# A gated linear recurrence with a tanh-shrink layer behind it: seven products for the second dense product, engine orders from a list scheduler, two heads computed in place for two units

## The chip, the cores and the metric

The kernel runs on one core of one Trainium2 chip. A core has five engines, each with an instruction queue of its own that it works off in order: TensorE (matmuls; in the profile PE, and PEld for its weight loads), VectorE (DVE), ScalarE (ACT), GpSimd (POOL) and SyncE (SP, which here only starts DMA transfers). TensorE writes its results into eight banks of PSUM; everything else lives in SBUF, with 128 partitions. The metric is the time of one execution on the device, in microseconds (us); the shorter, the better.

## What is computed

The reference has two stages. The first is a recurrence over 768 time steps for 4 batches and 8 heads with 48 features each; the second is a dense layer on the result.

```python
for t in range(S):                                   # S = 768, state is 48 x 48 per head
    state = alpha[t][:, None] * state + outer(k[t], v[t])
    y[t] = q[t] @ state
x = y, transposed to (3072 tokens, 384 features)     # 8 heads x 48
h = x @ w_in                                         # 384 x 2048
g = h - tanh(h)
out = g @ w_out                                      # 2048 x 384
```

q, k, v and alpha are 32-bit floats; w_in and w_out arrive as 64-bit floats. The output has 3072 x 384 32-bit floats.

## The kernel before

**Units and steps.** The 3072 tokens are cut into 12 units of 256 tokens; three units make up a batch. A unit has two chunks of 128 tokens. For every unit the kernel runs the recurrence (`gla`) and the dense layer (`moe`); the dense layer of a unit is cut into 8 steps of 256 hidden features each.

**The recurrence of a unit.** alpha, k and q are loaded (`load`, issued at line 362) so that VectorE can turn them with 32 x 32 transposes (`flip`, line 381) into tiles with features on the partitions: two heads share the 128 partitions, at partitions 0 to 47 and 64 to 111. A head's 48 features need two 32-partition blocks, so each tensor is loaded twice, the second time shifted by 32 elements. VectorE then makes two running products of the decays: a backward scan U (line 395) and a forward scan W (line 411), with some small operations in between (lines 403 to 405). GpSimd multiplies k by U and q by W (line 417), and ScalarE sums the squares of U and W as a check of their size (line 427). For each chunk TensorE multiplies q and k to scores (line 451), VectorE masks them (458), and TensorE makes y out of the old state and the masked scores (472, 476). ScalarE copies y into the layer's input xT (483, 484). xT has 384 rows without gaps, three blocks of 128. y's two-head groups fill only 96 of 128 partitions, so the rows of the last two heads go to a tile xs and from there, by six small DMA transfers (`moves`, line 523), into the gaps of the other three groups' rows. For the next chunk's state TensorE turns k back (492), ScalarE copies it (497), TensorE makes the update (503), GpSimd decays the old state (463), and VectorE adds both (512, or 510 in the first chunk of a batch).

**A step of the layer.** `first` (line 534) makes h for 256 hidden features and 256 tokens: six products with 128 x 128 weights and 256 columns, each two instructions. h - tanh(h) is a polynomial in u = h squared, which ScalarE and VectorE share: ScalarE makes u and two squares of linear functions of it (lines 542 to 544), VectorE w = h u, then z1 and g (545 to 547), and ScalarE accumulates how far u exceeds the range in which the polynomial is valid (549). `second` (line 558) multiplies g by w_out: for each of two feature blocks and two token chunks one product with 384 columns, summed over the 8 steps in two PSUM banks. At the unit's end ScalarE copies the two sums (564) and SyncE stores them. At the very end flags are checked; if a range was left, a slower general routine computes everything again.

**The weights.** They are loaded in 16 pieces (8 of w_in, 8 of w_out) of 768 columns, and rounded from 64 to 32 bits in `round_weight`: two ScalarE operations (lines 61, 62), three on VectorE (65, 67, 69) and one addition on GpSimd (72). At most four raw pieces are held at a time. Unit 0's steps can only run as pieces come in.

**What sets the order.** Every piece of work is put into a list with a time written out by hand (`put(at, ...)`): one table of times for unit 0, one for unit 1, one relative table for all others, and a step every 6.6 us. The list is sorted by these times, and the instructions are issued in that order; each engine's queue is thus fixed, and semaphores alone decide when an instruction runs. `first` of a step stands 2.5 steps ahead of its `second`.

**PSUM.** Two banks hold scores, one y, one the turned-back k and the update, two h, two the sums of `second`.

Of the kernel before, what the change touches and what calls it, by code (L numbers as in the profile page):

```python
# [8 lines left out]
FP32 = mybir.dt.float32  # L9
# [7 lines left out]
P = 128  # L17
HP = 64
# [239 lines left out]

def fast(tc, q, k, v, alpha, moe_w_in, moe_w_out, out, w_in, w_out, ident, ok, pad_rows):
# [11 lines left out]
    EV = HP + D  # L271
# [5 lines left out]
    with ExitStack() as ctx:  # L277
# [4 lines left out]
        ps_y = ctx.enter_context(tc.tile_pool(name="ps_y", bufs=1, space=PSUM))  # L282
        ps_h = ctx.enter_context(tc.tile_pool(name="ps_h", bufs=2, space=PSUM))
        ps_o = ctx.enter_context(tc.tile_pool(name="ps_o", bufs=1, space=PSUM))


# [10 lines left out]
        raws = [consts.tile([P, NP, R, D], FP32, name=n) for n in ("ar", "kr", "qr")]  # L297
        for t, x in zip(raws, (1.0, 0.0, 0.0)):
            V.memset(t[:, :, R - 1, :], x)


# [5 lines left out]
        for t in (after, before):  # L307
            GP.memset(t, 0.0)
        low = consts.tile([P, N], FP32, name="low")
        GP.memset(low, 1.0 / R_MAX)  # L310
        GP.memset(after[:, P::P + 1], 1.0)
        states = [consts.tile([P, NP, EV], FP32, name=f"state{i}") for i in range(2)]
# [3 lines left out]
        raw_in, raw_out = {}, {}  # L316

        def fetch_in(s):
            parts = []
            for i in range(len(pad_rows[0])):  # L320
                at, f0 = pad_rows[0][i]
                step = pad_rows[1][i][1] - f0
                src = moe_w_in[f0:f0 + KT * step].rearrange("(j p) n -> p j n", p=step)
                parts.append((at, src[0:at.stop - at.start, :, 2 * s * P:2 * (s + 1) * P]))
            raw_in[s] = load_weight(nc, two, parts)

        def fetch_out(s):
            raw_out[s] = load_weight(nc, two, [(slice(0, P), w_out_r[:, 2 * s:2 * s + 2, :])])

        def round_in(s):  # L330
            return round_weight(nc, two, raw_in.pop(s), w_in[:, :, 2 * s * P:2 * (s + 1) * P])

        def round_out(s):
            return round_weight(nc, two, raw_out.pop(s), w_out[:, 2 * s:2 * s + 2, :])


        plan = []

        def put(at, do, *args):
            plan.append((at, len(plan), do, args))  # L340

        def convert(at, make, s):

            it = []
            put(at, lambda: (it.append(make(s)), next(it[0])))
            put(at + 1, lambda: next(it[0]))
            put(at + 3, lambda: next(it[0], None))
# [3 lines left out]
        def load(u):  # L351
            b, i = divmod(u, UPB)
            t0 = i * TU
            other = A if u == 0 else nc.sync
            for n, (t, x) in enumerate(zip(raws, (alpha, k, q))):
                queue = other if n == 1 else nc.sync
                for hh in range(2):
                    src = x[b].rearrange("(g two) s d -> two g (s d)", two=2)[hh][:, t0 * D:(t0 + TU) * D]
                    src = src.rearrange("g (i n) -> i g n", i=32)
                    for dq in range(2):  # L360
                        at = 64 * hh + 32 * dq
                        queue.dma_start(
                            out=t[at:at + 32].rearrange("p g r d -> p g (r d)")[:, :, 0:R * D - 32 * dq],
                            in_=src[:, :, 32 * dq:])
            vt = vts[u] = three.tile([P, CU, H, D], FP32, name="vt")
            for c in range(CU):
                other.dma_start(out=vt[:, c], in_=v[b, :, t0 + c * P:t0 + (c + 1) * P, :].rearrange("h p d -> p h d"))

        def gla(u, at):

# [5 lines left out]
            m = {}  # L376

            def flip(raw, make):
                t = make()
                for g in range(NP):  # L380
                    V.transpose(t[:, g].rearrange("p c (i r) -> p r c i", r=R), raw[:, g, :, 0:32])  # L381
# [4 lines left out]

            put(at["aT"], flip, raws[0], lambda: tail[:, :, 0:P].rearrange("p (g c) t -> p g c t", c=CU))
            put(at["kT"], flip, raws[1], lambda: new("kT"))
            put(at["qT"], flip, raws[2], lambda: new("qT"))

# [6 lines left out]
            put(at["U"], scan_U)  # L397
# [8 lines left out]
            put(at["ends"], ends)  # L406
# [6 lines left out]
            put(at["W"], scan_W)  # L413

            def scale(name, by, cs):
                t = m[name][:, :, cs]
                GP.tensor_mul(t, t, m[by].rearrange("p (g c) t -> p g c t", c=CU)[:, :, cs, 1:])  # L417
            for name, by in (("kT", "U"), ("qT", "W")):
                if u == 0:
                    for c in range(CU):  # L420
                        put(at[name + by] + c, scale, name, by, slice(c, c + 1))
                else:
                    put(at[name + by], scale, name, by, slice(0, CU))
# [8 lines left out]
            def open_x():  # L432
                m["xs"] = two.tile([P, TU], FP32, name="xs")
                xT[u] = two.tile([P, KT, TU], FP32, name="xT")
# [253 lines left out]
```

## Time and profile before

| | |
|---|---|
| median of three runs | 719.04 us (716.86 to 722.59) |
| the profiled execution | 716.62 us |
| its span, first to last instruction | 714.8 us |
| TensorE's mean granted clock | 0.975 |
| busy: TensorE, VectorE, ScalarE, GpSimd | 621.6, 451.3, 329.2, 115.9 us |
| `first` (line 534), `second` (line 558) on TensorE | 275.8, 267.0 us |
| the scan W (line 411), the transposes (line 381) on VectorE | 48.7, 73.3 us |
| read and written in HBM | 44.43 and 4.72 MB |

The page of the profile gives busy times by engine, a picture of the span in 40 slices (each digit is the busy share in tenths), DMA queues, the chain of work that ended last, and groups of instructions. A group's row reads: line, engine, operation, what it writes and reads, shapes and count; then busy time in all and mean nanoseconds of one; then the idle time of the engine ahead of it and what ended that. A row of the timeline begins with the start and the duration in us; in brackets stands the idle time ahead of it and its releaser. Matmuls are pipelined: their rows overlap, and the distance from start to start is what they cost in a stream.

### The profile page before, as it was taken

Reading aid. Unit: us, or ns where it says so; the run is one execution under the profiler, and the core shown is the slowest. Engines: PE = TensorE matmul, PEld = TensorE weight load, DVE = VectorE, ACT = ScalarE, POOL = GpSimd, SP = SyncE. Lnnn points to the kernel's source line nnn. Section 1 sums busy time; section 2 is a strip of 40 time slices with the busy share of each in tenths; the row PEclk is TensorE's granted clock in tenths of the full one; section 3 lists DMA queues with packets and bytes.
Section 4 is the critical chain, followed back from the end, with each engine's and each line's share of the span. In section 5 each row is a group of like instructions: output and inputs, shape, how many; then the busy total and the mean of one; then the engine's idle time right before and its main releaser. Section 6 shows DMA issues by size and latency. Waiting matters only on the chain.

```text
span 714.8 us, 8728 instructions
## 1 busy us (share of the span) xinstructions
PE 621.6 (87%) x3089; PEld 460.4 (64%) x3089; DVE 451.3 (63%) x639; ACT 329.2 (46%) x701; POOL 115.9 (16%) x98
## 2 busy tenths in 40 slices
PE   0655586879989989989989989989989989989995
PEld 0543365657757767767767667767767767767773
DVE  4749877783683783682783773773874864874341
ACT  1435355544544544544634534634544444444451
POOL 2522543130020030030020120030110120120000
PEclk9978799999999999999999999999999999999998
DMA  9996556300801701701702602602603503500000
GB/s 181 213 178 146 107 141 164 58 1 18 160 1 28 150 1 31 146 1 37 141 1 55 122 1 54 124 1 60 118 1 81 97 1 81 98 0 7 23 0 28
DMA packets 57268, 50.99 MB, mean 71 GB/s; under 512 B 29440, under 2 KB 52096, under 8 KB 57216
## 3 DMA queue, kind: packets, MB, share of 16 engines
q1 hardware_dynamic: 54560, 49.20, 33.0%
q10 hardware_dynamic: 2656, 1.15, 1.0%
q8 instruction: 26, 0.43, 0.3%
q14 instruction: 26, 0.21, 0.1%
HBM read 44.43 MB, written 4.72 MB: 69 GB/s over the span
## 4 chain that ended last, share of the span: by engine, by line
PE 45%; DVE 27%; DMA 15%; POOL 5%; issue 3%; ACT 2%; SPq 2%; DVEq 0%; POOLq 0%; ACTq 0%
PE h L534 21%; PE o L558 15%; DVE W L411 6%; DMA qr<-in_q_dram 6%; DMA raw<-in_moe_w_in_dram 4%; DMA ar<-in_alpha_dram 3%; PE sc L451 3%; DVE kT L381 3%; DVE qT L381 3%; DVE z L546 3%; POOL qT L417 3%; DVE U L395 3%; PE y L476 3%; DVE w L545 3%; DVE aT L381 3%
## 5 line engine op out<-in xcount | busy, mean ns | idle before, releaser
L534 PE MATMUL h<-xT,w_in 128*128 128x256 f32 x1152 | 275.8, 391 | 22.9 <-POOL w_in L72 15.3
L558 PE MATMUL o<-w_out,g 128*128 128x384 f32 x768 | 267.0, 491 | 11.4 <-POOL w_out L72 11.4
L534 PEld LDWEIGHTS h<-xT,w_in 128*128 128x128 f32 x1152 | 221.7, 195 | 72.1 <-POOL w_in L72 17.6
L558 PEld LDWEIGHTS o<-w_out,g 128*128 128x128 f32 x768 | 144.3, 191 | 95.3 <-POOL w_out L72 13.1
L542 ACT ACTIVATE u<-h 128x512 f32<-128x512 f32 x96 | 57.3, 597 | 244.2 <-PE h L534 244.2
L545 DVE TENSOR_TENSOR w<-h,u 128x512 f32<-128x512 f32 x96 | 65.6, 683 | 162.6 <-ACT u L542 162.4
L417 POOL TENSOR_TENSOR kT<-kT,U 128x1024 f32<-128x1024 f32 (+1 forms) x13 | 30.3, 2331 | 377.1 <-DVE least L404 377.1
L546 DVE SCALAR_TENSOR_TENSOR z<-z,w 128x512 f32<-128x512 f32 x96 | 83.5, 869 | 10.6 <-DVE w L545 0.9
L547 DVE SCALAR_TENSOR_TENSOR g<-z,z 128x512 f32<-128x512 f32 x96 | 67.3, 701 | 10.4 <-ACT big L549 0.5
L543 ACT ACTIVATE z<-u 128x512 f32<-128x512 f32 x96 | 60.5, 630 | 3.1
L549 ACT ACTIVATE big<-u 128x512 f32<-128x512 f32 x96 | 58.9, 614 | 0.0
L544 ACT ACTIVATE z<-u 128x512 f32<-128x512 f32 x96 | 58.9, 613 | 0.0
L411 DVE TENSOR_TENSOR_SCAN W<-aT,before 128x1032 f32<-128x1032 f32 x12 | 48.7, 4059 | 0.4
L458 DVE TENSOR_TENSOR pm<-sc,mask 128x512 f32<-128x512 f32 x46 | 29.6, 685 | 16.9 <-PE sc L451 16.5
L503 PE MATMUL up<-vt,kn 128*128 128x96 f32 x160 | 22.8, 287 | 18.8 <-ACT kn L497 18.8
L417 POOL TENSOR_TENSOR qT<-qT,W 128x1024 f32<-128x1024 f32 (+1 forms) x13 | 26.7, 2053 | 65.6 <-DVE qT L381 65.6
L451 PE MATMUL sc<-qT,kT 48*128 48x128 f32 x368 | 27.6, 291 | 10.5 <-POOL qT L417 10.5
L451 PEld LDWEIGHTS sc<-qT,kT 48*128 48x128 f32 x368 | 23.1, 193 | 20.8 <-POOL qT L417 16.7
L503 PEld LDWEIGHTS up<-vt,kn 128*128 128x128 f32 x160 | 20.8, 198 | 22.6 <-ACT kn L497 22.0
L483 ACT COPY xs<-y 48x128 f32<-48x128 f32 x48 | 12.5, 260 | 46.5 <-PE y L476 46.2
L512 DVE TENSOR_TENSOR state<-state,up 48x192 f32<-48x192 f32 x32 | 11.2, 350 | 34.7 <-PE up L503 33.4
L492 PE MATMUL tp<-ident,kT 128*128 128x128 f32 x80 | 13.2, 291 | 20.1 <-POOL kT L417 20.1
(60 smaller groups left out, 444.0 us busy)
## 6 DMA issues: line engine op xcount, KB each, us to landing
raw<-in_moe_w_out_dram SPq DMA_DIRECT2D x8, 768.0 KB, 4.6
ar<-in_alpha_dram SPq DMA_DIRECT2D x24, 192.0 KB, 3.7
qr<-in_q_dram SPq DMA_DIRECT2D x24, 192.0 KB, 6.9
raw<-in_moe_w_in_dram SPq DMA_DIRECT2D x16, 288.0 KB, 7.8
out_dram<-ob SPq DMA_DIRECT2D x24, 192.0 KB, 1.9
ar<-in_alpha_dram SPq DMA_DIRECT2D x24, 176.0 KB, 4.1
qr<-in_q_dram SPq DMA_DIRECT2D x24, 176.0 KB, 6.9
kr<-in_k_dram SPq DMA_DIRECT2D x22, 192.0 KB, 5.3
```

The costliest lines, as they stand in the source:

```text
L381: V.transpose(t[:, g].rearrange("p c (i r) -> p r c i", r=R), raw[:, g, :, 0:32])
L411: V.tensor_tensor_scan(out=W.rearrange("p n t -> p (n t)"), data0=aT[:, 0:N * (P + 1)], data1=before, initial=0.0, op0=ALU.mult, op1=ALU.add)
L417: GP.tensor_mul(t, t, m[by].rearrange("p (g c) t -> p g c t", c=CU)[:, :, cs, 1:])
L451: T.matmul(sc[hh][:, g, :], lhsT=m["kT"][q, g, c, :], rhs=m["qT"][q, g, c, :], start=True, stop=True)
L534: T.matmul(h[:, a, :], lhsT=w_in[:, j, f * P:(f + 1) * P], rhs=xT[u][:, j, :], start=(j == 0), stop=(j == KT - 1))
L543: A.activation(z1, sq, AF.Square, bias=QB1, scale=QA)
L544: A.activation(z2, sq, AF.Square, bias=QB2, scale=QA)
L545: V.tensor_mul(w, h, sq)
L546: V.scalar_tensor_tensor(out=z1, in0=z1, scalar=QK1, in1=w, op0=ALU.add, op1=ALU.mult)
L547: V.scalar_tensor_tensor(out=g, in0=z2, scalar=QK2, in1=z1, op0=ALU.add, op1=ALU.mult)
L549: A.activation(big, sq, AF.Relu, bias=-U_MAX, accum_out=over[:, n:n + 1])
L558: T.matmul(o[c], lhsT=g[:, a * TU + c * P:a * TU + (c + 1) * P], rhs=w_out[:, f, :], start=(f == 0), stop=(f == FT - 1))
```

## The change

**Seven products.** For units 2 to 11, `second` uses Strassen's scheme on 2 x 2 blocks: g is cut by its two feature blocks and its two token chunks, w_out by feature block and by halves of its 384 columns. Seven products of 192 columns take the place of four of 384 (which are eight of 192). VectorE makes the five sums of blocks of g in three operations per step (`sums`, a tile e of 5 x 128 columns). The five combinations of blocks of w_out are made once (`combine`, four on GpSimd, one on VectorE, 1536 columns each), in memory that the raw weights had held, after the last piece has been converted. The products accumulate in four PSUM banks rather than two, and the store puts the output's blocks together: one copy on ScalarE, four operations on VectorE, four half-width stores. Units 0 and 1 (`PLAIN = 2`) keep the four products.

**Engine orders.** The hand-written times are gone. Each task has a name, an engine, an estimated duration, a rank and the tasks it waits for. `Planner.order` runs a list scheduling in Python while the kernel is built: always the engine that can start earliest takes, of its ready tasks, the one with the lowest rank. The order so found is the order of issue. A unit's dense steps have ranks 16 u + 2 s, their `second` 5 more; the recurrence of unit u begins at rank 16 u - 24 (units 0 and 1 at -40 and -20).

**In place.** For units 0 and 1 the rows of the last two heads are computed by TensorE straight into the gaps of y, with weight tiles of 32 columns that hold 16 features behind 16 zeros (`v_gap`, `s_gap`); one copy then takes y to xT, and `moves` and xs aren't used.

**Loads.** alpha, k and q are loaded once; the shifted second half is a copy from partition block to block (`widen`: six ScalarE copies per unit, for unit 0's alpha one of them on VectorE).

**PSUM.** y and the turned-back k and update lose their own banks. Units 0 and 1 use two of the four sum banks for them, later units the score banks, so that a chunk's scores wait until the chunk before has been masked, copied and added to the state.

**Smaller.** Unit 0's products of k with U and q with W go from GpSimd to VectorE; an early activation loads ScalarE's table; 36 and later 7 products of the identity matrix with itself keep TensorE busy ahead of its first work (`spin`).

The diff, cut to its core:

```diff
+class Planner:
...
+    def order(self):
...
+        while any(open_.values()):
+            at, engine = min((max(free.get(e, 0.0), min(ready[i] for i in ts)), e)
+                             for e, ts in open_.items() if ts)
+            i = min((i for i in open_[engine] if ready[i] <= at), key=lambda i: (self.tasks[i][3], i))
+            open_[engine].remove(i)
+            _, _, us, _, _, do, lat = self.tasks[i]
+            free[engine] = at + us
+            done.append((at, len(done), do, i))
+            for j in users[i]:
+                ready[j] = max(ready[j], at + us + lat)
...
+        RANK = {"in": -3, "out": 1}
+        def rank_moe(u):
+            return 2 * FS * u
+        def rank_gla(u):
+            return (-40, -20)[u] if u < 2 else 2 * FS * u - 24
...
+            add(f"read {what}{s}", "ACT", 1.85, rank, [f"fetch {what}{s}", older and f"{older[0]}{older[1]}"], a)
+            add(f"bits {what}{s}", "DVE", 2.6, rank, [f"read {what}{s}"], b)
+            add(f"{what}{s}", "POOL", 1.85, rank, [f"bits {what}{s}"], c)
...
-                    for dq in range(2):
-                        at = 64 * hh + 32 * dq
-                        queue.dma_start(
-                            out=t[at:at + 32].rearrange("p g r d -> p g (r d)")[:, :, 0:R * D - 32 * dq],
-                            in_=src[:, :, 32 * dq:])
...
+                queue.dma_start(out=t[HP * hh:HP * hh + 32].rearrange("p g r d -> p g (r d)"),
+                                in_=src.rearrange("g (i n) -> i g n", i=32))
...
+            def widen(what):
+                for hh in range(2):
+                    t, r0 = raws[what], HP * hh
+                    to, of = t[r0 + 32:r0 + HP, :, :, 0:D - 32], t[r0:r0 + 32, :, :, 32:D]
+                    if u == 0 and what == 0 and hh == 1:
+                        V.tensor_copy(to, of)
+                    else:
+                        A.copy(to, of)
...
+                (V if u == 0 else GP).tensor_mul(t, t, m[by][:, :, 1:])
...
+            go("W", "DVE", 2.6, 3, ["ends", prev and f"qW{prev}", prev and f"sizeW{prev}"], scan_W)
+            go("kU", *(("DVE", 1.3) if u == 0 else ("POOL", 2.4)), 3, ["kT", "U"], lambda: scale("kT", "U"))
...
+            def bank(name):
+                if direct:
+                    return ps_o.tile([P, NP, P], FP32, name=name, tag="o2" if name == "y" else "o3")
+                return ps_sc.tile([P, NP, P], FP32, name=name, tag="sc0" if name == "y" else "sc1")
...
+                    to_gap = [(hh, slice(HP * hh + D - gap, HP * hh + HP), j)
+                              for hh in range(2) for j in range(KT)] if direct else []
+                    if n == 0:
+                        for hh, at, j in to_gap:
+                            T.matmul(y[at, j, :], lhsT=v_gap[:, c, hh, j, :], rhs=m["pm", c][hh][:, NP - 1, :],
+                                     start=(j == 0), stop=True, skip_group_check=True)
...
+        def combine(n):
...
+            if n == 0:
+                GP.tensor_add(combos["11+22"], b11, b22)
...
+                def sums():
+                    g = m["g", s]
+                    e = m["e", s] = three.tile([P, 5, P], FP32, name="e")
+                    V.tensor_add(e[:, 0:2, :], g[:, 0], g[:, 1])
+                    V.tensor_sub(e[:, 2:4, :], g[:, :, 1, :], g[:, :, 0, :])
+                    V.tensor_add(e[:, 4, :], g[:, 0, 0, :], g[:, 1, 1, :])
...
+                    for n, i, g_, w_ in ((2, 1, e[:, 1, :], w[:, 0, 0]),
+                                         (1, 0, g[:, 1, 1, :], combos["21-11"][:, s]),
+                                         (1, 1, g[:, 0, 0, :], combos["12-22"][:, s]),
+                                         (2, 0, e[:, 0, :], w[:, 1, 1]),
+                                         (0, 0, e[:, 4, :], combos["11+22"][:, s]),
+                                         (3, 0, e[:, 3, :], combos["-21-22"][:, s]),
+                                         (3, 1, e[:, 2, :], combos["11+12"][:, s])):
+                        T.matmul(o[n][:, i], lhsT=g_, rhs=w_, start=(s == 0 and (n, i) in ((0, 0), (1, 0), (2, 1), (3, 0))),
+                                 stop=(s == FS - 1), skip_group_check=True)
...
+                add(f"first {me}", "PE", 2.75, r,
+                    [f"in{s}" if plain else None, f"cube {older[2]}" if older[2] else f"masked 0.{CU - 1}"]
...
+                    add(f"sums {me}", "DVE", 1.2, r + 1.1, [f"shrunk {me}"], sums)
+                add(f"second {me}", "PE", 2.75 if plain else 2.5, r + 5,
...
+                A.copy(p52, o[2])
+                V.tensor_sub(same, o[0][:, 0:1, :].to_broadcast([P, 2, NH]), p52)
+                V.tensor_add(same, same, o[1])
+                V.tensor_add(cross, p52, o[1][:, ::-1, :])
+                V.tensor_add(same, same, o[3])
...
+        add("spin 0", "PE", 9, -99, [], lambda: spin(36))
+        add("spin 1", "PE", 1.5, -20, [f"qT 0"], lambda: spin(7))
...
-            for _, _, do, args in sorted(plan, key=lambda x: x[:2]):
-                do(*args)
+            for _, _, do, _ in plan.order():
+                do()
```

448 lines of the change are left out of this document (287 added, 161 removed).

## Prediction

> **What bounds it now.** I read the page first, for the shares and the slices.
>
> ```profile
> span 714.8 us, 8728 instructions
> PE 621.6 (87%) x3089; PEld 460.4 (64%) x3089; DVE 451.3 (63%) x639; ACT 329.2 (46%) x701; POOL 115.9 (16%) x98
> PE   0655586879989989989989989989989989989995
> DVE  4749877783683783682783773773874864874341
> PEclk9978799999999999999999999999999999999998
> ```
>
> There are two regimes. For some seven slices (about 125 us) TensorE is half idle and VectorE is as busy as ever; from the ninth slice on TensorE is at nine tenths. So I asked for busy times by stretch: the first 135 us, one unit of the steady part, and the sum over eight units.
>
> ```profile
> 0.00:126.00 126.00, 70.21 (x341) 52.16 (x342) 89.41 (x119) 53.66 (x94) 48.31 (x43) 0.88 0.77 162
> 126.00:135.00 9.00, 6.74 (x27) 4.79 (x26) 6.55 (x8) 6.23 (x12) 1.80 (x1) 1.00 0.37 49
> ...
> 356.30:409.10 52.80, 50.22 (x257) 37.27 (x256) 34.06 (x50) 25.33 (x57) 5.34 (x5) 1.00 0.30 60
> ...
> sum 424.60, PE 403.92 PEld 300.26 DVE 271.79 ACT 201.45 POOL 51.58; mean PE 50.49 PEld 37.53 DVE 33.97 ACT 25.18 POOL 6.45
> ```
>
> The columns are the stretch, its length, then busy us (and instructions) of PE, PEld, DVE, ACT, POOL, then clock and DMA. The means of the sum row are per unit: a unit has 52.8 us (53.1 as the mean, 424.60/8; I reckon with 52.8), TensorE works 50.5 of them, VectorE 34.0, ScalarE 25.2. The steady part is TensorE's, with about 2.5 us per unit lost. The timeline of one unit shows where that goes and what a step costs:
>
> ```profile
> 362.18 1.13 PE L503 MATMUL up<-vt,kn 128*128 128x96 f32 x8 [1.61 <-ACT kn L497]
> 366.89 1.16 PE L451 MATMUL sc<-qT,kT 48*128 48x128 f32 x16 [0.97 <-POOL qT L417]
> 386.04 1.03 PE L503 MATMUL up<-vt,kn 128*128 128x96 f32 x8
> 386.90 2.77 PE L558 MATMUL o<-w_out,g 128*128 128x384 f32 x8
> 389.51 2.75 PE L534 MATMUL h<-xT,w_in 128*128 128x256 f32 x12
> 392.10 2.74 PE L558 MATMUL o<-w_out,g 128*128 128x384 f32 x8
> 394.68 2.75 PE L534 MATMUL h<-xT,w_in 128*128 128x256 f32 x12
> ```
>
> The durations overlap, so I use distances between starts. The first product takes 392.10 - 389.51 = 2.59 us for twelve instructions of 256 columns (0.216 each), the second 394.68 - 392.10 = 2.58 for eight of 384 (0.323 each): 0.84 us per thousand columns in both. The recurrence's products wait for ScalarE and GpSimd (1.61 and 0.97); the dense ones don't wait at all.
>
> **Second product.** Per step four 384-column products (eight instructions) become seven of 192 columns (fourteen). At the same rate that is 14 x 0.1625 = 2.28 us, 0.30 us less; 2.4 us per unit of eight steps, for ten units. TensorE's work falls from 50.5 to 48.1 us per unit. The unknown is whether fourteen weight loads keep up. The "up" rows start 386.90 - 386.04 = 0.86 us apart for eight loads of 128 columns, so one load can follow another within 0.107 us, under 0.1625: hidden. A group row reads otherwise:
>
> ```profile
> L558 PEld LDWEIGHTS o<-w_out,g 128*128 128x128 f32 x768 | 144.3, 191 | 95.3 <-POOL w_out L72 13.1 <-issue 1.8
> L403 DVE TENSOR_TENSOR ends<-U,low 128x8 f32<-128x8 f32 x12 | 1.9, 162 | 0.0
> L497 ACT COPY kn<-tp 128x512 f32<-128x512 f32 x20 | 11.5, 575 | 23.2 <-PE tp L492 23.2
> ```
>
> A load is listed with 191 ns, but as a duration beside running matmuls; the 0.107 spacing is the harder bound, and I take no cost.
>
> [...]
>
> **What VectorE gets.** Three sums per step (256, 256 and 128 elements), and four 384-element operations in each unit's store.
>
> ```profile
> 377.89 0.69 DVE L545 TENSOR_TENSOR w<-h,u 128x512 f32<-128x512 f32 x1 [4.09 <-ACT u L542]
> 378.68 0.69 DVE L546 SCALAR_TENSOR_TENSOR z<-z,w 128x512 f32<-128x512 f32 x1
> 379.48 0.69 DVE L547 SCALAR_TENSOR_TENSOR g<-z,z 128x512 f32<-128x512 f32 x1
> 380.09 1.28 DVE L458 TENSOR_TENSOR pm<-sc,mask 128x512 f32<-128x512 f32 x2
> ...
> 402.36 2.31 DVE L395 TENSOR_TENSOR_SCAN U<-aT,after 128x1032 f32<-128x1032 f32 x1
> ```
>
> From 8 elements in 0.162 us and 512 in 0.69, an element costs 1.05 ns and an instruction 0.154 us. The sums are then 0.42 + 0.42 + 0.29 = 1.13 us per step, 9.0 per unit; the store 4 x 0.56 = 2.2. VectorE goes from 34.0 to 45.2 us per unit, against TensorE's 48.1. That is the heart of the case: TensorE's work shrinks by 2.4 us and VectorE's grows by 11.2, until they are nearly equal. And GpSimd costs VectorE more:
>
> ```profile
> 356.13 2.17 POOL L417 TENSOR_TENSOR kT<-kT,U 128x1024 f32<-128x1024 f32 x1 [38.66 <-DVE least L404]
> 356.29 4.18 DVE L411 TENSOR_TENSOR_SCAN W<-aT,before 128x1032 f32<-128x1032 f32 x1
> 364.67 2.17 POOL L417 TENSOR_TENSOR qT<-qT,W 128x1024 f32<-128x1024 f32 x1 [6.37 <-DVE qT L381]
> 365.22 2.17 DVE L546 SCALAR_TENSOR_TENSOR z<-z,w 128x512 f32<-128x512 f32 x1
> ```
>
> The scan W has the length of U (2.31) and takes 4.18 beside a GpSimd product; z takes 2.17, not 0.69. Such stalls are inside the 34.0 already, but the sums read SBUF only, as z does, and will meet more of GpSimd's 6.45 us per unit: 0 to 2 more, so 45 to 47. The scheduler's list gives W 2.6 us, first 2.75, second 2.5; it plans on a VectorE with more room than these rows leave it.
>
> What a period becomes: not under 48.1. Today's list loses about 2.5 us in places a scheduler can mend (products queued ahead of their inputs), but the slack is thinner: between a first product and its second stand two firsts and two seconds, 2 x (2.59 + 2.28) = 9.7 us, and the chain square, quadratics, two VectorE steps and sums needs about 0.6 + 1.3 + 1.6 + 1.1 = 4.6 of them before any queueing. I take 51.2, TensorE's floor and 3.1 of waiting, a little more than now, in a span of 48.6 to 55. That is 1.6 x 10 = 16 us gained.
>
> **The opening.** Here the conversion of the weights (three VectorE and one GpSimd instruction for each of 16 pieces) sets the pace.
>
> ```profile
> 1.16 1.82 SPq L362 DMA_DIRECT2D ar<-in_alpha_dram  x4
> 10.75 2.02 DVE L381 STREAM_TRANSPOSE aT<-ar 128x256 f32<-128x256 f32 x4 [9.21 <-DMA ar<-in_alpha_dram]
> 44.69 10.98 PE L534 MATMUL h<-xT,w_in 128*128 128x256 f32 x36 [7.66 <-DMA xT<-xs]
> 50.82 0.69 DVE L545 TENSOR_TENSOR w<-h,u 128x512 f32<-128x512 f32 x1 [8.91 <-ACT u L542]
> 83.52 0.56 DVE L67 TENSOR_SCALAR mag<-mag 128x768 int32<-128x768 int32 x1
> ...
> 85.22 1.98 POOL L72 TENSOR_TENSOR w_in<-mag,last 128x768 int32<-128x768 int32 x1 [6.08 <-DVE mag L69]
> 85.58 2.04 DVE L67 TENSOR_SCALAR mag<-mag 128x768 int32<-128x768 int32 x1
> 132.57 1.80 POOL L72 TENSOR_TENSOR w_out<-mag,last 128x768 int32<-128x768 int32 x1 [6.72 <-DVE mag L69]
> ...
> ar<-in_alpha_dram SPq DMA_DIRECT2D x24, 192.0 KB, 3.7
> ...
> ar<-in_alpha_dram SPq DMA_DIRECT2D x24, 176.0 KB, 4.1
> ```
>
> VectorE is busy 89.41 + 6.55 = 96 us of the 135 that end with the last conversion, so 39 are idle. Part by part:
> (a) Loads without the second, shifted copy: 384 KB per tensor, not 736. Alpha and k together took 10.75 - 1.16 = 9.6 us; 9.6 x 384/736 = 5.0 by bytes alone, a gain of 4.6, less two widening copies of about 0.58 (the 512-column ScalarE copy): 3 us.
> (b) y in place for units 0 and 1: no moves, hence no 7.66 us wait for a transfer queued behind weight pieces. VectorE's 8.91 us wait at 50.82 has this and the slow clock behind it; matmuls of 32-column weights replace it, about 1 us of TensorE time that nothing else wants here. I take 9 of VectorE's idle time as usable; bounds 0 (the next piece isn't there either) and 9. The warming matmuls run before TensorE's first work and only serve this.
> (c) List order: 39 - 9 - 9 = 21 us of idle left, of which I give it 6, bounds 0 and 15.
> (d) Unit 0's two scalings go to VectorE: 2 x 1.23 = 2.5 us, less the scan's stall; cost 2.
> Sum 3 + 9 + 6 - 2 = 16 us earlier, bounds 1 and 25.
>
> **The combinations of w_out.** Four GpSimd sums of 1536 elements, at 2.17 us per 1024 3.25 each, 13 in all, and one VectorE operation of 1.8. They fall into unit 1, where VectorE idles some 19 us in 53; they also stand ahead of unit 2's scalings on GpSimd, whose slack (the recurrence's ranks run at least three steps ahead of its use) is larger. Bounds 0 and 13, the row at 365.22 being the nearest: it passes one stall on to VectorE and none to TensorE. I take 4.
>
> [...]
>
> **The rest.** Widening adds 6 x 0.575 = 3.5 us of ScalarE per unit to 25.2: hidden by its idle half; uncovered it would be 3.5 per unit. Such a copy waits for its load with the next squares queued behind it; the load is issued some four steps ahead and lands in about 4 us (the rows 3.7 and 4.1), so nothing here either. SyncE issues fewer loads, but four half stores instead of two, and the loads behind them wait for VectorE's sums; they are due about four steps ahead, so nothing. y, tp and up move into the two score banks, so a chunk's scores now wait until the chunk before has been read: some 8 us of chain per chunk, under half a unit for both; nothing, unless the recurrence falls late. The end: a 384-column copy and four VectorE operations follow the last product, 0.48 + 2.2, where two copies did:
>
> ```profile
> 706.45 0.48 ACT L564 COPY ob<-o 128x384 f32<-128x384 f32 x1 [4.70 <-PE o L558]
> 707.09 0.48 ACT L564 COPY ob<-o 128x384 f32<-128x384 f32 x1 [0.17 <-PE o L558]
> ```
>
> 2.7 instead of 1.1: cost 1.5.
>
> **Sum.** The profiled execution took 716.62 us (span 714.8); the median of the runs is 719.04, 0.3% above, less than the runs differ. 716.6 - 16 (opening) + 4 (combinations) - 16 (units) + 1.5 (end) = 690.
>
> **Rivals.** Forecast, period 50 to 52.5: 678 to 703, chance 0.45.
> The combinations' 13 us of stalls all reach TensorE: 690 + 9 = 699, 0.05; z's stretch speaks for it, VectorE's 19 idle us against.
> Scheduler fills nearly all: period 48.6, opening 25 earlier, combinations free: 716.6 - 25 - 42 + 1.5 = 651. For: dense products never wait now, and VectorE idles 39 us in the opening. Against: VectorE at 45 to 47 of 48.6. 0.20.
> VectorE becomes the bound, the slower side. While it does the front of the recurrence (about 13 us) it also owes three steps of 2.2 + 1.1; 23 us, 27 if both GpSimd products block it, against 3 x 4.87 + 2.2 = 16.8 of TensorE and a slack of 5.1 (9.7 - 4.6). TensorE then waits up to 5 us per unit beside other losses: period 55, 716.6 - 10.5 + 22 = 728. It decides from a period of 53.9, where the 10.5 us of the other terms are used up. For: 94% occupancy; against: lag can be made good in the rest of the unit. 0.13.
> Weight loads of 191 ns don't overlap: 14 x 0.191 = 2.67 per step, 0.09 more than now, period 53.9, about 717; against it the 0.107 spacing. 0.05.
> The opening stays, because conversions alternate between VectorE and GpSimd (2.04 at 85.58 for 0.56 at 83.52): 716.6 + 4 - 16 + 1.5 = 706, the rest of the sum holding. 0.12.
>
> About 1% (7 us) is what can be told from no change. Below 712 lie the forecast, the two cases after it and most of the last: 0.77. Within 1%: loads, and the edges of forecast and last: 0.10. Above 726: 0.13. The range 650 to 718 leaves out VectorE's case and the lower edge of the scheduler's.
>
> **What would show it.** Starts of second products 2.28 us before the next first in pairs; a period of 50 to 52.5 with VectorE busy 45 to 47; first dense product near 34 us (44.7 less 7.7 and 3), last conversion ended near 118 (134.4 less 16); z and the sums stretched to 2 to 3 us beside the combinations. The forecast is wrong if second steps take over 2.5 us, if TensorE waits for "e" more than 3 us per unit, or if the last conversion stays past 130.

## The result, and the profile after

The changed kernel takes 656.47 us (median of four runs, 654.76 to 657.52), against 718.7 us before (four runs, 716.86 to 722.59): a ratio of 0.9125 with a 95% interval of 0.9081 to 0.917. Forecast were 690 us and a range of 650 to 718, so the direction held and the size did not: 62 us gained where 29 were forecast. The time lies inside the range, near its lower edge. The profiled execution is the one of 654.76 us, with a span of 653.0; before it was 716.62 and 714.8.

The page after, its shares and slices:

```profile
span 653.0 us, 10271 instructions
PE 614.9 (94%) x3723; PEld 536.7 (82%) x3723; DVE 547.0 (84%) x927; ACT 368.9 (56%) x761; POOL 127.3 (19%) x100
PE   7889966969999999999999999999999999999994
DVE  7999999999959979879899799689899656565862
```

VectorE's row has turned: from the second slice to the eleventh it is full, then at seven to nine tenths with few exceptions, and at five or six toward the end, where it had been at three to eight in nearly every slice. TensorE has a nine in every slice from the tenth to the last but one. Busy times by stretch, with the columns of the prediction, show both parts:

```profile
0.00:126.00 126.00, 102.88 (x576) 76.18 (x578) 119.22 (x157) 79.34 (x140) 57.58 (x48) 0.92 0.69 151
126.00:135.00 9.00, 4.69 (x34) 3.73 (x30) 8.90 (x4) 1.35 (x5) 5.87 (x2) 0.91 0.31 89
219.60:506.00 286.40, 285.92 (x1834) 261.84 (x1833) 254.54 (x464) 168.70 (x360) 39.22 (x33) 1.00 0.17 41
219.60:600.40 380.80, 380.26 (x2430) 348.39 (x2429) 313.49 (x583) 213.20 (x460) 42.24 (x39) 1.00 0.14 34
```

The last row runs from the start of unit 3 to that of unit 11 (units are found by counting the products of `first` through the timeline). TensorE is idle for 0.54 us in 381; a unit takes 380.80/8 = 47.6 us (its period, from its start to the next one's), and TensorE's work in it is 380.26/8 = 47.5. The same count before:

```profile
235.80:553.90 318.10, 302.42 (x1545) 224.91 (x1544) 203.51 (x291) 150.83 (x335) 39.12 (x32) 1.00 0.30 61
235.80:660.40 424.60, 403.32 (x2062) 300.20 (x2061) 271.70 (x391) 200.92 (x446) 53.36 (x44) 1.00 0.28 57
```

There a unit takes 53.1 us with 50.4 of work. The chain of work that ended last (after each start, how long it held the chain) has the new product in it, in step with the first:

```profile
255.49 2.28 PE o L774 x14
257.77 2.59 PE h L715 x12
260.36 2.28 PE o L774 x14
```

Where the 61.8 us of span went: unit 2 starts at 171.0 instead of 183.0 (12.0 us), and from there to the end it takes 482.0 instead of 531.8 (49.8 us). In the latter, ten units bring 51.1 and the end costs 1.3: the last `second` ends 9.0 us before the end (at 643.99; one of its four banks is copied from 643.05 on), where it was 7.7.

### The profile page after: what moved, and what is told of

Same layout as the page of the kernel before. It is cut to its first block, busy times and chain, and to the rows that moved or that the text cites. A ratio compares the mean times of both kernels' runs of the same rounds, so it can differ in the third digit from the quotient of the medians.

```text
span 653.0 us, 10271 instructions
## 1 busy us (share of the span) xinstructions
PE 614.9 (94%) x3723; PEld 536.7 (82%) x3723; DVE 547.0 (84%) x927; ACT 368.9 (56%) x761; POOL 127.3 (19%) x100
## 4 chain that ended last, share of the span: by engine, by line
PE 72%; DVE 19%; issue 4%; ACT 2%; DMA 1%; POOL 0%; SPq 0%; DVEq 0%; POOLq 0%; ACTq 0%
PE h L715 31%; PE o L774 26%; PE y L598 3%; PE sc L557 3%; PE o L759 2%; PE y L588 2%; PE up L622 2%; DVE z L735 2%; DVE g L736 2%; DVE mag L67 2%; DVE qT L478 2%; DVE mag L65 1%; DVE w L730 1%; DVE kT L478 1%; DVE mag L69 1%
## 5 line engine op out<-in xcount | busy, mean ns | idle before, releaser
L736 DVE SCALAR_TENSOR_TENSOR g<-z,z 128x512 f32<-128x512 f32 x96 | 95.4, 993 | 10.0
L774 PE MATMUL o<-b,e 128*128 128x192 f32 x480 | 91.1, 326 | 0.0
L774 PE MATMUL o<-w_out,e 128*128 128x192 f32 x320 | 80.7, 334 | 0.0
L774 PEld LDWEIGHTS o<-b,e 128*128 128x128 f32 x480 | 80.2, 190 | 0.0
L774 PE MATMUL o<-b,g 128*128 128x192 f32 x320 | 65.1, 326 | 0.0
L774 PEld LDWEIGHTS o<-w_out,e 128*128 128x128 f32 x320 | 56.5, 190 | 6.6 <-issue 2.8
L759 PE MATMUL o<-w_out,g 128*128 128x384 f32 x128 | 48.8, 528 | 8.0 <-DVE g L736 7.9
L774 PEld LDWEIGHTS o<-b,g 128*128 128x128 f32 x320 | 54.2, 190 | 0.0
L759 PEld LDWEIGHTS o<-w_out,g 128*128 128x128 f32 x128 | 25.6, 206 | 25.1 <-POOL state L567 6.7
L747 DVE TENSOR_TENSOR e<-g 128x256 f32<-128x256 f32 x80 | 33.2, 416 | 1.4
```

Source lines behind the costliest of these rows:

```text
L736: V.scalar_tensor_tensor(out=g.rearrange("p a c t -> p (a c t)"), in0=z2, scalar=QK2, in1=z1, op0=ALU.add, op1=ALU.mult)
L747: V.tensor_add(e[:, 0:2, :], g[:, 0], g[:, 1])
L759: T.matmul(m["o"][c], lhsT=g[:, a, c, :], rhs=w_out[:, f, :], start=(f == 0), stop=(f == FT - 1))
L774: T.matmul(o[n][:, i], lhsT=g_, rhs=w_, start=(s == 0 and (n, i) in ((0, 0), (1, 0), (2, 1), (3, 0))), stop=(s == FS - 1), skip_group_chec ...
```

## The experiments

Two theories were set against each other. One says that the new order is the gain and the seven products a small part of it. Its rival says that the products are, with the order only making room for them. The second question was why TensorE doesn't wait, though VectorE has so much more to do.

**The order without the seven products.** All units make the four products; no sums, no combinations, everything else as in the changed kernel.

```diff
-        for n in range(5):
-            add(f"combine {n}", ...
-            plain = u < PLAIN
+            plain = True
```

> Four products of 384 columns in every unit, no sums and no combinations; list order and everything else as in the changed kernel. Theory A (the order took the waits away, the seven products only took 0.30 us per step off TensorE, and the two add up): a unit takes 47.3 + 2.4 = 49.7 us in the steady part, TensorE still without waits, and the time is 656 + 24 = 680, less up to 4 for the combinations. Theory B (the seven products also made room elsewhere, or the list order does well only with them): a period over 51 and 690 or more.

It took 670.53 us, 0.9334 [0.9287, 0.938]. Busy times from unit 3 to unit 9 and to unit 11:

```profile
214.10:514.50 300.40, 300.40 (x1546) 225.54 (x1545) 201.06 (x295) 167.48 (x364) 45.22 (x32) 1.00 0.15 38
214.10:613.50 399.40, 399.40 (x2046) 300.04 (x2045) 239.41 (x355) 212.48 (x467) 48.25 (x38) 1.00 0.12 31
```

TensorE has no idle time at all, and a unit takes 399.40/8 = 49.9 us, as the first theory had it (49.7). The time is below its 676 to 680, since the opening is shorter too. Unit 2 starts at 164.2, and from there to the end are 503.9 us. So the order, together with the other parts (single loads, y in place, `spin`, banks), brings 18.8 us in the opening and 27.9 after it. The seven products then bring 21.9 us after unit 2's start (503.9 - 482.0, some 2.3 per unit) and cost 6.8 before it (171.0 - 164.2): 48 of 62 us are not theirs.

**The seven products without the order.** All of the changed kernel's work, issued by the old table of times; new tasks stand next to those that they serve. Beside it the same with four products.

```diff
-            for _, _, do, _ in plan.order():
+            for _, _, do, _ in by_hand():
                 do()
```

> All of the changed kernel's instructions, but issued in the order of the hand-written times of the kernel before (new tasks put beside their neighbours: sums behind g, widening 1.5 us ahead of the transposes, combinations behind the last conversion). Theory A: TensorE keeps the waits of the kernel before, 2.5 us per unit or more since VectorE is fuller, so a period of 50 to 53, and the opening loses most of its 13 us: 690 to 705. Theory B (the seven products alone bring the steady gain, the order is of little weight): a period of 47.3 to 48.5 and at most 675.

> The list kernel with four products in every unit, issued in the order of the hand-written times of the kernel before. With seven products that order gave a period of 60.8 us and 782. Theory A (that order fails because of the seven products: the sums in VectorE's queue and the store that the next unit's first product waits for): a period of 52.5 to 54 and about 715. Theory B (it fails because y and the update now share the score banks, which that order was not made for): 56 or more, and over 745.

Both are slower than the kernel before: 782.01 us (1.0871 [1.0819, 1.0923]) and 749.14 us (1.0413 [1.0372, 1.0455]), with periods of 60.5 and 57.5 us. With seven products that is beyond what either theory allowed; with four it is in the second one's bounds. The waits of TensorE with seven products, in all, times, and longest, then the busy times from unit 3 to 11:

```profile
PE o L774 <- DVE cross L812: 38.6, 9, 4.8
PE sc L557 <- DVE state L630: 15.5, 7, 2.9
```

```profile
245.90:729.60 483.70, 419.87 (x2447) 379.71 (x2446) 335.90 (x615) 229.47 (x486) 53.38 (x44) 0.93 0.15 32
```

and one of those waits in the timeline:

```profile
257.02 0.48 ACT L809 COPY p<-o 128x384 f32<-128x384 f32 x1
259.76 2.02 DVE L478 STREAM_TRANSPOSE kT<-kr 128x256 f32<-128x256 f32 x4
261.63 0.53 DVE L810 TENSOR_TENSOR same<-o,p 128x384 f32<-128x384 f32 x1
263.27 1.65 PE L774 MATMUL o<-b,g 128*128 128x192 f32 x4 [4.79 <-DVE cross L812]
```

The store's operations hold the four sum banks. By the old times they stand in VectorE's queue behind a later unit's transposes, and the next unit's `second` waits 4.79 us for the banks. The second row of the waits is the shared score banks. By the old times a chunk's update stands ahead of its own scores (15.5 and 18 in the table), both use one bank, and so the scores wait until VectorE has added the update to the state; the list puts the scores first. With four products there is no such store. TensorE's waits from unit 3 to 11 are then 39.3 us in 459.7, the two largest:

```profile
PE tp L613 <- POOL kT L513: 12.0, 7, 1.7
PE sc L557 <- DVE state L630: 10.3, 6, 1.8
```

The score banks have 13.5 of the 39.3 us (the second row, and 3.2 at line 628). Nearly all of the rest is for kT, qT and the turned-back k, which come late from GpSimd and ScalarE; which of the kernel's other parts delays them wasn't separated, so the second theory's cause is shown for a third of the waiting only. The prediction costed the shared banks at nothing "unless the recurrence falls late"; by the old times it is the place of the update that makes them cost. The list is therefore not one gain beside others: the store and the shared banks need an order made for them.

**The kernel before, with five times moved.** If its 2.5 us of waiting per unit were only a matter of places, later places must remove them.

```diff
-   ... sizeW=12, scores=(18, 27), masked=(20, 29), ... back=(13, 30), update=(15.5, 33), ...
+   ... sizeW=16, scores=(20, 27), masked=(21.5, 29), ... back=(14.5, 30), update=(18.5, 33), ...
```

> The kernel before with only five numbers of its hand-written table changed: back 13 to 14.5, update 15.5 to 18.5, scores 18 to 20, masked 20 to 21.5, sizeW 12 to 16. If its 2.4 us of waiting per unit came from products queued ahead of their inputs, a unit falls from 52.8 to about 50.5 us and the time to 694 to 702. If they came from VectorE being late whatever the place, the period stays above 52 and the time above 710.

691.77 us, 0.963 [0.9585, 0.9675]: 27 us for five numbers, and a period of 50.4. TensorE's waits from unit 2 on in the kernel before:

```profile
PE up L503 <- ACT kn L497: 12.5, 9, 1.6
PE sc L451 <- POOL qT L417: 9.6, 9, 1.4
```

and with the five times moved:

```profile
PE sc L451 <- POOL qT L417: 2.5, 9, 0.3
```

The first is gone and of the second a quarter is left. The steady part's gain by order can thus be had by hand in the old kernel: from unit 2's start to the end of the span it takes 507.6 us (689.5 - 181.9), near the 503.9 of the list. The opening's isn't in it, since unit 2 starts at 181.9.

**More for VectorE.** The first of the three sums is made twice, or three times, in each step of units 2 to 11, into the same place, with the order unchanged. This asks how full VectorE may be before TensorE waits.

```diff
                     V.tensor_add(e[:, 0:2, :], g[:, 0], g[:, 1])
+                    V.tensor_add(e[:, 0:2, :], g[:, 0], g[:, 1])
```

> The changed kernel with its first sum of 256 columns computed twice in every step of units 2 to 11, order unchanged: 8 x 0.42 = 3.4 us more VectorE work per unit, 45.3 instead of 41.9, the load that the prediction had reckoned with. If a VectorE that full makes TensorE wait, as the prediction's period of 51.2 had it: a period of 49 to 51 and 670 to 690. If VectorE costs nothing as long as its work is under TensorE's: 47.3 and 655 to 659.

> The changed kernel with its first sum computed three times per step of units 2 to 11: 6.7 us more VectorE work per unit than in the changed kernel, 39.2 + 6.7 = 46 of some 47.6 us, the upper end of what the prediction had expected VectorE to do. The first doubling cost 7.7 us in all (1.2 us of period, from 47.6 to 48.8). Theory A (waits grow with VectorE's load, so the prediction's 51.2 was right for the load it assumed and wrong in that load): a period of 50.5 to 52 and 680 to 695. Theory B (the waits stay small up to the point where VectorE is full): under 49.5 and at most 672.

664.14 us (0.9237 [0.9195, 0.928]) and 686.2 us (0.9538 [0.9495, 0.9582]). Busy times from unit 3 to unit 9, with the sum twice:

```profile
219.40:514.40 295.00, 288.96 (x1833) 262.55 (x1832) 274.41 (x511) 169.14 (x360) 40.20 (x33) 0.99 0.17 40
```

and three times, with the wait that it makes:

```profile
221.00:537.30 316.30, 294.60 (x1835) 266.88 (x1834) 296.02 (x564) 168.67 (x360) 40.19 (x33) 0.98 0.15 38
```

```profile
PE o L776 <- DVE e L749: 16.0, 10, 2.2
```

Divided by six units:

| | VectorE busy per unit | period |
|---|---|---|
| changed kernel | 42.4 us | 47.7 us |
| first sum twice | 45.7 | 49.2 |
| first sum three times | 49.3 | 52.7 |

At 42.4 us VectorE costs nothing; 3.3 us more cost 1.4, and the next 3.6 cost 3.5. TensorE then waits for "e", the wait that the prediction named, though 16.0 us in ten units is under the 3 us per unit that it set. The whole with the sum twice stays under the 670 us that were expected for this period.

These means hide that the units differ. VectorE's busy time and the unit's time, one by one:

| unit | changed kernel | first sum twice | three times |
|---|---|---|---|
| 3 | 44.4 of 49.0 us | 47.9 of 53.0 | 53.9 of 59.6 |
| 4 | 39.9 of 47.1 | 43.2 of 47.2 | 43.7 of 47.5 |
| 5 | 44.0 of 47.4 | 47.1 of 49.1 | 53.8 of 55.8 |
| 6 | 42.5 of 48.4 | 45.5 of 49.2 | 47.3 of 51.3 |
| 7 | 39.7 of 47.0 | 43.2 of 47.1 | 44.8 of 47.6 |
| 8 | 44.1 of 47.5 | 47.5 of 49.4 | 52.6 of 54.5 |

Units 4 and 7 stay under 45 us of VectorE and lose at most 0.6 us. In units 5 and 8 with the sum three times VectorE, its stalls included, is busy for longer than TensorE has work and in all but 2 us of the unit: there it is the bound.

**The combinations on VectorE.** All five, not only the last.

```diff
-                GP.tensor_add(combos["11+22"], b11, b22)
+                V.tensor_add(combos["11+22"], b11, b22)
...
-            add(f"combine {n}", "POOL" if n < 4 else "DVE", 3.6 if n < 4 else 1.9, 2 * FS + 2 + n,
+            add(f"combine {n}", "DVE", 1.9, 2 * FS + 2 + n,
```

> The changed kernel with all five combinations of w_out on VectorE (some 1.7 us each) instead of four on GpSimd (3.4 to 3.9 each). With four products unit 2 begins at 164.2 us, with seven at 171.0. If that comes from GpSimd's 15 us holding VectorE off, unit 2 begins at 165 to 168 and the time falls to 651 to 654. If it comes from the sums and the waiting for the last combination, or if VectorE has no 6.8 us to spare there: 656 or more.

650.7 us, 0.9051 [0.9022, 0.9079]: the fastest version, ahead of both kernels, and unit 2 starts at 163.4 instead of 171.0, earlier than the 165 to 168 that were expected. The timeline of the changed kernel has GpSimd's combinations beside VectorE's work:

```profile
124.60 3.44 POOL L684 TENSOR_TENSOR b<-w_out 128x1536 f32<-128x1536 f32 x1
124.92 3.67 DVE L735 SCALAR_TENSOR_TENSOR z<-z,w 128x512 f32<-128x512 f32 x1
128.00 3.87 POOL L686 TENSOR_TENSOR b<-w_out 128x1536 f32<-128x1536 f32 x1
128.69 3.73 DVE L736 SCALAR_TENSOR_TENSOR g<-z,z 128x512 f32<-128x512 f32 x1
```

and with all on VectorE:

```profile
122.87 1.74 DVE L682 TENSOR_TENSOR b<-w_out 128x1536 f32<-128x1536 f32 x1
```

A combination done by VectorE costs it 1.74 us; one done by GpSimd costs VectorE some 3 us, since z and g take 3.7 where they take 0.69. Moving work off VectorE here takes more of VectorE. In the stretch of 126 to 135 us of the changed kernel VectorE is busy 8.90 of 9 us with four instructions, and TensorE works 4.69 us. The scores wait there for an addition to the state, which stands behind these four at 135.16:

```profile
136.01 2.04 PE L557 MATMUL sc<-qT,kT 48*128 48x128 f32 x14 [5.32 <-DVE state L630]
```

With all combinations on VectorE the same scores run at 130.07 without a wait.

**Two scalings more on VectorE.** Beside the combinations, unit 1's products of k with U and q with W too.

```diff
-                (V if u == 0 else GP).tensor_mul(t, t, m[by][:, :, 1:])
+                (V if u <= 1 else GP).tensor_mul(t, t, m[by][:, :, 1:])
```

> The kernel with all combinations on VectorE (650.7), and unit 1's two scalings on VectorE too (1.2 us each there, where GpSimd takes 2.2 each and holds VectorE off meanwhile). If the same exchange holds as for the combinations, unit 2 begins 1 to 3 us earlier than at 163.4 and the time is 648 to 650; if VectorE, busy throughout the opening, has the longer way of it: 651 to 653.

656.73 us, 0.9127 [0.9098, 0.9157]: 6 us worse than without, and outside both cases that were expected. Unit 1 starts at 119.3 instead of 111.6, the last conversion ends at 127.9 instead of 120.6, and TensorE waits most for unit 0's g:

```profile
PE o L759 <- DVE g L736: 14.6, 3, 6.1
```

With the combinations alone that row has 8.7 us in all. The two tasks shift the list well beyond their own place, the conversions among the rest. Which of the exchanges makes unit 1 late stays open.

**The opening, part by part.** Three kernels, each with one part undone: the double loads in the place of `widen`; units 0 and 1 through xs and `moves`, in the score banks; no `spin`.

```diff
+                for dq in range(2):
+                    at = HP * hh + 32 * dq
+                    queue.dma_start(out=t[at:at + 32]...[:, :, 0:R * D - 32 * dq], in_=src[:, :, 32 * dq:])
```

> The changed kernel with alpha, k and q loaded twice again, the second time shifted, and no widening copies on ScalarE (the planner counts them as 0.01 us). The prediction gave the single loads 3 us, in the opening alone. By that: 659 to 660, the first dense product near 40 instead of 37.0, the steady part unchanged. If the loads hold up the weight pieces too: 664 or more. If ScalarE's six copies per unit cost more than the loads: under 656.

```diff
-            direct = u < PLAIN
+            direct = u < DIRECT    # DIRECT = 0
```

> The changed kernel with units 0 and 1 treated like the others: y through xs and six small transfers, y and the update in the score banks. The prediction gave the in-place y up to 9 us of the opening. By that: the first dense product near 45 instead of 37.0, unit 1's first step 5 to 9 us later than 112.1, 661 to 666. If VectorE's conversions set the pace of the opening whenever the first product starts: unit 1's first step within 3 us of 112.1 and 656 to 659.

```diff
-        add("spin 0", "PE", 9, -99, [], lambda: spin(36))
-        add("spin 1", "PE", 1.5, -20, [f"qT 0"], lambda: spin(7))
```

> The changed kernel without its 43 warming products. TensorE then runs its first products at the low clock; the prediction gave the warming nothing of its own. If VectorE sets the opening's pace: 655 to 658, unit 1's first step within 1 us of 112.1. If the early products are on the path: 659 to 662.

| | time | ratio | first dense product | last conversion ends | unit 1 | unit 2 |
|---|---|---|---|---|---|---|
| changed kernel | 656.47 us | 0.9125 [0.9081, 0.917] | 37.0 | 120.7 | 112.1 | 171.0 |
| double loads | 665.9 | 0.9256 [0.9217, 0.9296] | 36.2 | 130.0 | 120.8 | 181.3 |
| moves for units 0, 1 | 660.27 | 0.9176 [0.9139, 0.9214] | 65.2 | 100.8 | 121.6 | 176.7 |
| no `spin` | 658.36 | 0.915 [0.9111, 0.9189] | 39.0 | 123.7 | 115.3 | 174.2 |

The last two intervals overlap that of the changed kernel; that these parts gain something rests on the profiled executions, where unit 2 starts 5.7 and 3.2 us later without them.

The first dense product says little about the opening: with moves it comes 28 us later, and the whole takes 3.8 us more; with double loads it comes earlier, and the whole takes 9.4 more. Nor does the last conversion set the pace by itself. With moves it ends 20 us earlier, and yet unit 1 starts 9.5 us later:

```profile
98.98 1.83 POOL L72 TENSOR_TENSOR w_out<-mag,last 128x768 int32<-128x768 int32 x1 [2.15 <-DVE mag L69]
```

With double loads the conversion is kept waiting by bytes, at least in part: a weight piece lands after 8.3 us in the median instead of 6.1, and ScalarE waits 7.3 us for pieces instead of 3.6. The DMA's slices of the changed kernel:

```profile
DMA  9996770104003003003004014022020000010001
```

and with double loads:

```profile
DMA  9999985225603403405206106215111010010001
```

The DMA engines are then full or nearly so for six slices, not three, while weight pieces are still to come.

## Why the prediction was wrong in size

**The step that failed is the period.** It said "I take 51.2, TensorE's floor and 3.1 of waiting, a little more than now". TensorE's floor was nearly right: 48.1 forecast, 47.5 measured, and 2.4 us less than the 49.9 of the kernel with four products, as forecast. The 3.1 us of waiting are the error: TensorE is idle for 0.54 us in eight units. The prediction knew that the old 2.5 us were a matter of places, and five numbers moved in the old table took most of them away; but then it put 3.1 us in their place for a thinner slack, without a row that shows such a wait. 3.6 us in ten units are 36 us, and the forecast was 35 us too high against the profiled execution (690 against 654.8).

**Beneath it was, in part, VectorE's load.** "VectorE goes from 34.0 to 45.2 us per unit", with stalls 45 to 47; measured are 254.54/6 = 42.4. Two terms made the difference. One is a mistake of reading: for TensorE the prediction took distances between starts, for VectorE durations. VectorE's rows overlap too:

```profile
309.94 0.42 DVE L747 TENSOR_TENSOR e<-g 128x256 f32<-128x256 f32 x1
310.27 0.42 DVE L748 TENSOR_TENSOR e<-g 128x256 f32<-128x256 f32 x1
310.61 0.28 DVE L749 TENSOR_TENSOR e<-g 128x128 f32<-128x128 f32 x1
310.81 2.03 DVE L478 STREAM_TRANSPOSE qT<-qr 128x256 f32<-128x256 f32 x4
```

The sums are listed with 0.42, 0.42 and 0.28 us, just as forecast, but stand 0.33, 0.34 and 0.20 apart: 0.87 per step, not 1.13. The store's four are 0.47 apart by the same overlap of 0.08. Together that is 8 x 0.87 + 4 x 0.47 = 8.8 per unit where 11.2 was forecast; the changed kernel has 42.4 - 33.5 = 8.9 more than the one with four products. The prediction's own rows showed it: z at 378.68 and g at 379.48 are 0.69 long, but pm follows g after 0.61. The other term is the stalls, "0 to 2 more": W, z and g together take no longer than before, the stalls only lie elsewhere. Groups of the kernel before, over the span:

```profile
L411 DVE TENSOR_TENSOR_SCAN W<-aT,before 128x1032 f32<-128x1032 f32 x12 | 48.7, 4059 | 0.4
L546 DVE SCALAR_TENSOR_TENSOR z<-z,w 128x512 f32<-128x512 f32 x96 | 83.5, 869 | 10.6 <-DVE w L545 0.9
L547 DVE SCALAR_TENSOR_TENSOR g<-z,z 128x512 f32<-128x512 f32 x96 | 67.3, 701 | 10.4 <-ACT big L549 0.5
```

and after:

```profile
L508 DVE TENSOR_TENSOR_SCAN W<-aT,before 128x1032 f32<-128x1032 f32 x12 | 28.1, 2338 | 0.0
L735 DVE SCALAR_TENSOR_TENSOR z<-z,w 128x512 f32<-128x512 f32 x96 | 73.7, 768 | 4.8 <-ACT z L726 2.0
L736 DVE SCALAR_TENSOR_TENSOR g<-z,z 128x512 f32<-128x512 f32 x96 | 95.4, 993 | 10.0
```

In the new order GpSimd's products lie beside g and the small operation `ends` instead of W: 48.7 + 83.5 + 67.3 = 199.5 us become 197.2, and `ends` goes from 1.9 us in all to 10.2.

**The price put on such a load was too dear as well.** By the table of more sums, 45.7 us of VectorE give a period of 49.2 and 49.3 give 52.7, so 45 to 47 lie at 49 to 50.5, not at 51.2. From the 47.7 of these units that is 1.3 to 2.8 us for the load and 0.7 to 2.2 for the price. A load read by distances, 34 + 8.8 = 43, might have led nearer to the floor, and so to "Scheduler fills nearly all" (651, 0.20), which is what happened in the units; that is argued, not shown.

**The opening** came out at the 12 us that were forecast (16 less 4 for the combinations), but by terms that cancel; that the number fits is luck. Single loads were put at 3 us, for alpha's wait; undoing them costs 9.4, at least in part through the weight pieces. y in place was put at 9; undoing it costs 3.8. Its products with 32-column weights were put at about 1 us and take 5.1 in unit 0 (27.25 to 28.32 and 31.50 to 35.51). The warming matmuls are worth 1.9 by the medians, which is within the intervals: without them the sixteen score products at 24.98 us take 2.08 us, with them those at 25.10 take 1.16. The combinations were put at 4, in bounds of 0 to 13, and cost 6.8 by one pair of kernels and 5.8 by the other (656.47 - 650.7). These are undone one by one and needn't add up. Two signposts held nearly, from the timeline:

```profile
36.95 5.45 PE L715 MATMUL h<-xT,w_in 128*128 128x256 f32 x24 [0.58 <-ACT xT L604]
118.62 2.12 POOL L72 TENSOR_TENSOR w_out<-mag,last 128x768 int32<-128x768 int32 x1 [3.37 <-ACT big L742]
```

37.0 for "near 34", and the last conversion ended at 120.7 for "near 118". VectorE's idle 39 us before 135 became 7 (119.22 + 8.90 of 135): 32 were filled, where 15 were to be used.

Beside GpSimd's combinations of 3.44 and 3.87 us, VectorE's z and g took 3.67 and 3.73 us instead of 0.69. The prediction left open, in bounds of 0 to 13 us, how much of such stalls TensorE waits for; in the opening it waits 5.32 us in one piece.

**The rivals.** Weight loads of 191 ns are refuted: fourteen instructions in 2.28 us, 0.163 each, though their group still lists the loads near that:

```profile
L774 PEld LDWEIGHTS o<-b,e 128*128 128x128 f32 x480 | 80.2, 190 | 0.0
```

The busy share of the weight loads rose from 64% to 82% while the time fell by 62 us; what the loads cost is told by the distances. In that rival's price 0.09 us in eight steps are 0.7 us per unit, a period of 53.5 and not 53.9. VectorE as the bound (728) isn't seen in the changed kernel; it is seen in single units of the kernel with the first sum made three times, where VectorE is busy for 52.6 us and more. With the old order VectorE is part of the picture, but as a place in a queue that keeps banks from coming free, not as 94% of occupancy. Of the combinations' 13 us of stalls some six or seven reached TensorE, and the opening did not stay.

**The end** was put at 1.5 us and costs 1.3.

## What to carry to other kernels

Take distances between starts for every engine, not only for TensorE: on VectorE 0.08 us per instruction of overlap was a quarter of the sums' price. Look at a second engine's load unit by unit: with the first sum made twice, a mean of 45.7 us hid units of 47 to 48 that lost 1.7 to 4.0 us and others that lost 0.1. Judge a new order and the work that it makes possible by separate runs, since here the order and the opening's parts gave 48 of 62 us, and the new work under the old order was slower than before. Before a few operations are given to GpSimd to spare VectorE, compare what the stall costs VectorE with what the operation itself would.

## What was not expected of the hardware

A wait of TensorE was paid twice here. With the first sum made three times, one wait of 4.14 us at 223.8 to 227.9 is followed by slow products. Busy times of that place, the granted clock being the third number from the end:

```profile
222.00:226.00 4.00, 1.76 (x9) 1.20 (x7) 3.93 (x7) 0.60 (x1) 2.17 (x1) 1.00 0.35 98
228.00:232.00 4.00, 4.00 (x26) 3.76 (x28) 3.69 (x9) 2.25 (x5) 0.00 (x0) 0.50 0.02 4
232.00:234.00 2.00, 2.00 (x11) 1.64 (x8) 1.83 (x4) 1.31 (x5) 0.00 (x0) 0.57 0.00 0
```

The clock is half for nearly seven us (its mean is 0.73 in 226 to 228, between the first two rows). The wait need not be that long. In the same run one of 1.83 us, at 275.15 to 276.98, is followed by 3.4 us at half the clock, and one of 2.15 us, at 330.83 to 332.98, is not:

```profile
275.15:278.10 2.95, 1.12 (x8) 1.12 (x8) 2.85 (x7) 2.74 (x6) 0.00 (x0) 1.00 0.00 0
278.10:281.50 3.40, 3.40 (x12) 3.22 (x11) 3.26 (x8) 0.00 (x0) 0.00 (x0) 0.50 0.00 0
330.80:336.00 5.20, 2.57 (x15) 2.25 (x14) 5.03 (x12) 3.59 (x7) 0.00 (x0) 1.00 0.00 0
```

In the steady part of the kernel before, whose waits were at most 1.6 us, the clock was 1.00 throughout. With four products by the old order the longest wait was 2.6 us, and the clock was 0.97 as a mean. With seven products by the old order it was 0.93 as a mean, and TensorE was busy 419.87 us from unit 3 to 11 where the changed kernel needs 380.26 for the same work: of the 103 us by which that stretch is longer, 40 are slower products and the rest is waiting. So a wait cost its own length or about twice that, and its length alone doesn't tell which; what decides isn't shown by these runs.
